# A gated recurrence and a soft mixture of experts: an overlapping last token group, constants and a reciprocal moved later, and a hidden layer in four tiles

## The chip, the cores and the metric

One NeuronCore of a Trainium2 chip. The metric is device time of one execution in microseconds (us). A run over 1.5% above the fastest of its kernel counts as slow. In the views, PE is TensorE, PEld its weight loads, DVE VectorE, ACT ScalarE, POOL GpSimd and SP the queue that issues the loads; PEclk is the clock that TensorE was granted, in tenths of full speed, one digit for each of 40 slices of the span.

## The reference

```python
# x, f_logit: [4, 5056, 256] float32; lower_bound: [256]; phi: [256, 32]; w1: [8, 256, 1024]; w2: [8, 1024, 256]
f = lb + (1 - lb) * sigmoid(f_logit)
h = f[:, t] * h + (1 - f[:, t]) * x[:, t]        # over 5056 tokens, y[:, t] = h
logits = y @ phi                                  # y as 20224 tokens
slot_input = softmax(logits, axis=0).T @ y        # 32 slots, 4 per expert
slot_out[e] = relu(slot_input[e] @ w1[e]) @ w2[e]
out = softmax(logits, axis=1) @ slot_out
```

## The kernel before

Each batch's 5056 tokens are cut into ten groups of 512 (4 tokens a partition, 128 partitions); a group of one batch is a unit, so there are 40. 5056 is 9 x 512 + 448, so the last group fills 112 partitions. Per unit: two loads; a sigmoid (`gate`, ScalarE); its product with x (`enter`, GpSimd); transposes of both (TensorE); the decay (ScalarE); two scans, the recurrence itself (VectorE); transposes back. Groups are exponentiated and gathered into slots in pairs, the last two alone. Expert weights are loaded by GpSimd's queue between its products. In the experts' layer, slot_sb holds the gathered slots, sin the slots made ready for the experts, hi_ps the products of the hidden layer, ht_ps their transposes, so_ps the products of the second layer and slot_out its result.

```python
def rows(g):
    return min(P, (S - g * G) // R)          # 128, and 112 for the last group
# ... constants: ident goes twice through TensorE; rep and phi on VectorE, all ahead of the loop
def load(n):
    g, b = divmod(n, B); n_p = rows(g)
    nc.sync.dma_start(out=fs[n][:n_p], in_=f_logit[b, ds(g * G, n_p * R)]...)   # x_t likewise
# ... the loop over n; in it, in this order on their engines:
    unit(decay, n + 1); group(exps, n - 2); unit(gate, n + 3)      # ScalarE
    unit(enter, n + 3); load_w(...)                                # GpSimd
    unit(to_tokens, n - 1); unit(s_to_channels, n + 2); unit(u_to_channels, n + 1)   # TensorE
    unit(scan, n); ...; group(row_sums, n - 4)                     # VectorE; row sums on GpSimd
nc.vector.tensor_copy(slot_sb, slot_ps)
nc.vector.reciprocal(rrow, rsum)
# ... experts' layer
for q in range(E // Q):
    hi_ps = pbig.tile([P, F], F32, tag=f"hi_ps{q}")                # both halves, one tile
    for k in range(2):
        # 8 matmuls into hi_ps[..., half k]
        if k == 0: nc.scalar.activation(hi[half 0], hi_ps[half 0], ACT.Relu)
        else:      nc.vector.tensor_scalar_max(hi[half 1], hi_ps[half 1], 0.0)
```

The softmax here doesn't subtract the row's maximum and nothing guards it: scores larger than these inputs give would overflow.

## Time and profile before

| | before |
|---|---|
| time, median of 4 runs | 219.65 us (219.25 to 221.96) |
| span of the profiled run | 218.2 us |
| last x load landed | 132.7 us |
| last scan starts | 137.79 us |
| last weight landed | 150.4 us |
| experts' layer, slot_sb to slot_out | 145.69 to 160.54 us |

Times in the second half are from the span's start, in the profiled run. The loads' row carries the first stage, the rows from slot_sb to slot_out a chain in which nearly every instruction waits for the one before, and the output is again a DMA stage. The lines themselves stand in the prediction.

Three measurements of this trace behind the prediction. The page counts 8.39 MB for the 16 weights, 2 bytes an element; of the 58.23 MB read from HBM, 41.42 are the loads of x and f_logit, and the other 16.8 match the weights' float32 size. The packet times of all queues, the weights' among them, sum to 1.01 to 1.07 of the 16 engines in each stretch of 4 us from 112 to 148 us. And unit 35's product ended at 117.33, but its transposes started at 121.92, behind those of unit 36's sigmoid (121.12).

### The profile page before, as it was taken

To read this page: it belongs to the slowest core of one execution; us is meant where nothing else is said; L and a number is where in the kernel's file an instruction comes from. 1 tells how busy PE (TensorE), PEld (TensorE's weight loads), DVE (VectorE), ACT (ScalarE), POOL (GpSimd) and SP (SyncE) were. 2 spreads that over 40 slices of the span, in tenths; PEclk is the share of its full clock that TensorE was granted. 3 is DMA by queue.
4 is the path that set the end of the run, shared out by engine and by line. 5 is a ranking of instruction groups with operands and counts; after the bars stand their busy time and mean duration, and the time that the engine had idled before them with its cause. 6 is when DMAs were issued, how large, how long until landed. Compare 5 with 4: busy or idle time off the path is not lost. (4 is left out here: it accounts for less than half of the span.)

```text
span 218.2 us, 3088 instructions
## 1 busy us (share of the span) xinstructions
PE 133.0 (61%) x1042; PEld 90.8 (42%) x1042; DVE 152.3 (70%) x165; ACT 137.1 (63%) x220; POOL 109.7 (50%) x93
## 2 busy tenths in 40 slices
PE   0386637456664776658573793665958778667600
PEld 0275525355553555556452762432733323223300
DVE  0779998909999899989998297533168446465530
ACT  3499556898889989998787858012034554245520
POOL 1379667359993999969983789742000000000000
PEclk9999999969999999999999589555595555555555
DMA  6999999999999999999999999992009999999995
GB/s 200 414 413 411 321 415 333 404 413 341 390 381 357 414 318 420 320 417 338 399 317 267 243 232 213 197 213 59 5 23 405 405 405 407 400 405 405 405 356 187
DMA packets 19696, 70.76 MB, mean 324 GB/s; under 512 B 2464, under 2 KB 2464, under 8 KB 19680
## 3 DMA queue, kind: packets, MB, share of 16 engines
q1 hardware_dynamic: 17088, 62.14, 74.6%
q0 software_dynamic: 2304, 8.39, 19.2%
q8 instruction: 8, 0.13, 0.2%
q10 hardware_dynamic: 288, 0.03, 0.1%
q14 instruction: 8, 0.07, 0.1%
HBM read 58.23 MB, written 20.71 MB: 362 GB/s over the span
## 5 line engine op out<-in xcount | busy, mean ns | idle before, releaser
L150 POOL TENSOR_TENSOR u_t<-s_t,x_t 128x1024 bf16<-128x1024 bf16 (+1 forms) x39 | 83.4, 2152 | 32.6 <-ACT s_t L144 14.2
L184 DVE TENSOR_TENSOR_SCAN h<-a,h,up 128x512 bf16<-128x512 f32 (+1 forms) x72 | 86.5, 1248 | 0.4 <-PE up L157 0.2
L144 ACT ACTIVATE s_t<-f_t 128x1024 bf16<-128x1024 f32 (+1 forms) x40 | 42.6, 1065 | 18.2 <-DMA f_t<-in_f_logit_dram 18.0
L174 ACT ACTIVATE a<-sp,nomlb 128x512 f32<-128x512 bf16 (+1 forms) x80 | 50.2, 685 | 3.9 <-PE sp L157 3.6
L195 PE MATMUL hp<-ident_f,h 128*128 128x128 f32 (+1 forms) x160 | 30.7, 317 | 34.6 <-DVE ht L204 25.5
L420 ACT ACTIVATE ob<-op,rrow 128x256 f32<-128x256 f32 (+1 forms) x64 | 25.1, 474 | 30.2 <-DVE ob L414 13.1
L414 DVE TENSOR_TENSOR ob<-op,rrow 128x1024 f32<-128x1024 f32 (+1 forms) x24 | 29.0, 1223 | 19.5 <-DMA out_dram<-ob 16.2
L195 PEld LDWEIGHTS hp<-ident_f,h 128*128 128x128 f32 (+1 forms) x160 | 22.6, 208 | 45.5 <-DVE ht L204 34.4
L408 PE MATMUL op<-slot_out,etall 32*128 32x256 bf16 (+1 forms) x160 | 33.9, 379 | 12.4 <-ACT ob L420 7.7
L157 PE MATMUL sp<-ident_f,s_t 128*128 128x128 f32 (+1 forms) x160 | 26.7, 296 | 10.2 <-ACT s_t L144 9.8
L408 PEld LDWEIGHTS <-etall 32*128 32x128 bf16 (+1 forms) x160 | 15.4, 130 | 30.9 <-issue 27.7
L157 PE MATMUL up<-ident_f,u_t 128*128 128x128 f32 (+1 forms) x160 | 26.2, 291 | 2.8 <-POOL u_t L150 2.8
L157 PEld LDWEIGHTS sp<-ident_f,s_t 128*128 128x128 f32 (+1 forms) x160 | 20.5, 155 | 11.9 <-ACT s_t L144 11.0
L157 PEld LDWEIGHTS up<-ident_f,u_t 128*128 128x128 f32 (+1 forms) x160 | 20.5, 153 | 3.4 <-POOL u_t L150 3.3
L204 DVE COPY ht<-hp 128x512 f32<-128x512 f32 (+1 forms) x30 | 20.0, 666 | 1.8 <-PE hp L195 1.8
L243 DVE COPY et<-ep 128x1024 bf16<-128x1024 bf16 (+2 forms) x6 | 3.6, 602 | 15.3 <-PE ep L240 15.3
L184 DVE TENSOR_TENSOR_SCAN h<-a,up 128x512 bf16<-128x512 f32 x8 | 9.1, 1202 | 1.5 <-PE up L157 1.5
L228 ACT ACTIVATE etall<-lg 128x1024 bf16<-128x1024 f32 (+2 forms) x6 | 5.2, 872 | 7.2 <-PE lg L219 7.1
L262 POOL TENSOR_TENSOR rs<-rs 128x128 f32<-128x128 f32 (+6 forms) x18 | 7.9, 442 | 1.4
L144 ACT ACT_TABLE_LOAD x5 | 6.4, 1283 | 3.1 <-PEq L439 1.7
L262 POOL TENSOR_TENSOR rs<-et 128x512 f32<-128x512 bf16 (+2 forms) x6 | 6.0, 998 | 3.8 <-DVE et L243 3.8
L270 PE MATMUL slot_ps<-ht,et 128*32 128x256 bf16 (+1 forms) x160 | 7.4, 314 | 0.6 <-DVE et L243 0.6
(89 smaller groups left out, 92.0 us busy)
## 6 DMA issues: line engine op xcount, KB each, us to landing
f_t<-in_f_logit_dram SPq DMA_DIRECT2D x36, 512.0 KB, 12.5
x_t<-in_x_dram SPq DMA_DIRECT2D x36, 512.0 KB, 12.5
out_dram<-ob SPq DMA_DIRECT2D x36, 512.0 KB, 5.6
f_t<-in_f_logit_dram SPq DMA_DIRECT2D x4, 448.0 KB, 15.6
x_t<-in_x_dram SPq DMA_DIRECT2D x4, 448.0 KB, 16.2
out_dram<-ob SPq DMA_DIRECT2D x4, 448.0 KB, 6.0
w_sb_105<-in_moe_w_dram POOLq DMA_DIRECT2D x1, 512.0 KB, 8.6
w_sb_106<-in_moe_w_dram POOLq DMA_DIRECT2D x1, 512.0 KB, 8.1
```

The costliest lines, as they stand in the source:

```text
L144: nc.scalar.activation(sts[n][:n_p], fs.pop(n)[:n_p], ACT.Sigmoid, scale=-1.0)
L150: eng.tensor_tensor(uts[n][:n_p], sts[n][:n_p], xs.pop(n)[:n_p], ALU.mult)
L157: nc.tensor.transpose(ps[:, :n_p, r], t[:n_p, r], ident_f[:n_p, :n_p])
L174: nc.scalar.activation(a[:, :T], sp[:, :T, o], ACT.Identity, scale=nomlb[:, ds(o, 1)], bias=1.0)
L184: nc.vector.tensor_tensor_scan(h[:, :T, o], decays.pop((n, o))[:, :T], up[:, :T, o], hs[n - B][:, ds(G - 1, 1), o] if n >= B else 0.0, ALU ...
L195: nc.tensor.transpose(hp[:n_p, r], hw[:, :n_p, r], ident_f)
L204: copy(hts[g][:n_p, b].rearrange("p r d -> p (r d)").bitcast(F32), hps.pop(n)[:n_p].rearrange("p r c -> p (r c)"))
L262: nc.gpsimd.tensor_tensor(dst, part[:, :, :w], part[:, :, ds(w, w)], ALU.add)
L270: nc.tensor.matmul(slot_ps[ds(b * NS, NS), :], et[:n_p, r, b], ht[:n_p, b, r], start=(g == 0 and r == 0), stop=(g == n_grp - 1 and r == R ...
L408: nc.tensor.matmul(op[:n_p, r], ew[ds(b * NS, NS), :, r], slot_out[ds(b * NS, NS), :], start=True, stop=True, skip_group_check=True)
L414: nc.vector.tensor_tensor(ob[:n_p], op[:n_p], rrow[:n_p, g, :, ds(b, 1)].broadcast_to([n_p, R, D]), ALU.mult)
L420: nc.scalar.activation(ob[:n_p, r], op[:n_p, r], ACT.Copy, scale=rrow[:n_p, g, r, ds(b, 1)])
```

## The change

The intent: let the last group start at token 4544, overlapping the one ahead by 64 tokens, so that every load fills 128 partitions (of the group ahead only 448 tokens are used); start the first unit before the constants are built; move the reciprocal off the chain; and give each half of the hidden layer a tile of its own. The core of the diff:

```diff
+    def first(g):
+        return g * G if g < n_grp - 1 else S - G
+    def used(g):
+        return first(g + 1) - first(g) if g < n_grp - 1 else G
     def rows(g):
-        return min(P, (S - g * G) // R)
+        return used(g) // R
 ...
-                in_=f_logit[b, ds(g * G, n_p * R)]...        # n_p = rows(g)
+                in_=f_logit[b, ds(first(g), n_p * R)]...     # n_p = P; x_t, gate, enter, transposes, scan likewise
 ...
-                    hs[n - B][:, ds(G - 1, 1), o] if n >= B else 0.0,
+                    hs[n - B][:, ds(used(n // B - 1) - 1, 1), o] if n >= B else 0.0,
 ...
-    # word, word_t: ident by two transposes on TensorE, ahead of the loop
+            if n == -3: lb_constants()          # two small operations
+            if n == 1:  other_constants()       # ident, four copies of rep, two of phi, on VectorE
 ...
-    nc.vector.reciprocal(rrow, rsum)            # ahead of the experts' layer
+        nc.vector.reciprocal(rrow, rsum)        # behind the copies of the transposed hidden layer
 ...
-            hi_ps = pbig.tile([P, F], F32, name="hi_ps", tag=f"hi_ps{q}")
             for k in range(2):
+                hi_ps = pbig.tile([P, H], F32, name="hi_ps", tag=f"hi_ps{q}{k}")
```

More of the change, by code (lines that the diff above doesn't have):

```diff
@@ L50 @@
     make_identity(nc, ident_f)
-    word = consts.tile([P, P, 2], BF16, name="word")
-    nc.vector.memset(word.rearrange("p c o -> p (c o)"), 0.0)
-    nc.vector.tensor_copy(word[:, :, 0], ident_f)
-    word_t = consts.tile([P, P, 2], BF16, name="word_t")
     ident = consts.tile([P, P], BF16, name="ident")
-    with tc.tile_pool(name="psi", bufs=1, space=PSUM) as psi:
-        ip = psi.tile([P, P], F32, name="ip")
-        iw = psi.tile([P, P], F32, name="iw")
-        w_f = word.bitcast(F32).rearrange("p c o -> p (c o)")
-        wt_f = word_t.bitcast(F32).rearrange("p c o -> p (c o)")
-        nc.tensor.transpose(ip, w_f, ident_f)
-        nc.scalar.copy(wt_f, ip)
-        nc.tensor.transpose(iw, wt_f, ident_f)
-        nc.vector.tensor_copy(wt_f, iw)
-        nc.vector.tensor_copy(ident, word_t[:, :, 0])
     rep = consts.tile([P, B, NS], F32, name="rep")
-    for b in range(B):
-        blk = ident_f[ds(b * NS, NS), ds(b * NS, NS)]
-        nc.vector.tensor_copy(rep[ds(b * NS, NS)],
-                              blk.unsqueeze(1).broadcast_to([NS, B, NS]))
     lb = consts.tile([P, DC], F32, name="lb")
@@ L77 @@
     omlb = consts.tile([P, DC], F32, name="omlb")
-    nc.vector.tensor_scalar(omlb, lb, -1.0, 1.0, ALU.mult, ALU.add)
     nomlb = consts.tile([P, DC], F32, name="nomlb")
-    nc.vector.tensor_scalar(nomlb, lb, 1.0, -1.0, ALU.mult, ALU.add)
     phi_f = consts.tile([P, DC, NS], F32, name="phi_f")
@@ L83, with lb_constants, other_constants @@
     phi = consts.tile([P, DC, NS], BF16, name="phi")
-    for o in range(DC):
-        nc.vector.tensor_scalar_mul(phi[:, o], phi_f[:, o], omlb[:, ds(o, 1)])
+    def lb_constants():
+        nc.vector.tensor_scalar(omlb, lb, -1.0, 1.0, ALU.mult, ALU.add)
+        nc.vector.tensor_scalar(nomlb, lb, 1.0, -1.0, ALU.mult, ALU.add)
+    def other_constants():
+        nc.vector.tensor_copy(ident, ident_f)
+        for b in range(B):
+            blk = ident_f[ds(b * NS, NS), ds(b * NS, NS)]
+            nc.vector.tensor_copy(rep[ds(b * NS, NS)],
+                                  blk.unsqueeze(1).broadcast_to([NS, B, NS]))
+        for o in range(DC):
+            nc.vector.tensor_scalar_mul(phi[:, o], phi_f[:, o], omlb[:, ds(o, 1)])
     store = ctx.enter_context(tc.tile_pool(name="store", bufs=1))
@@ L129, in load @@
             g, b = divmod(n, B)
-            n_p = rows(g)
+            n_p = P
             fs[n] = ld.tile([P, R, D], F32, name="f_t", tag="f_t")
@@ L133, in load @@
                 out=fs[n][:n_p],
-                in_=f_logit[b, ds(g * G, n_p * R)].rearrange("(p r) d -> p r d", r=R))
+                in_=f_logit[b, ds(first(g), n_p * R)].rearrange("(p r) d -> p r d", r=R))
             xs[n] = ld.tile([P, R, D], F32, name="x_t", tag="x_t")
@@ L137, in load @@
                 out=xs[n][:n_p],
-                in_=x[b, ds(g * G, n_p * R)].rearrange("(p r) d -> p r d", r=R))
+                in_=x[b, ds(first(g), n_p * R)].rearrange("(p r) d -> p r d", r=R))
         def gate(n):
-            n_p = rows(n // B)
+            n_p = P
             sts[n] = sup.tile([P, R, D], BF16, name="s_t", tag="s_t")
@@ L146, in enter @@
         def enter(n):
-            n_p = rows(n // B)
+            n_p = P
             uts[n] = sup.tile([P, R, D], BF16, name="u_t", tag="u_t")
@@ L152, in to_channels @@
         def to_channels(n, src, dst, tag):
-            n_p = rows(n // B)
+            n_p = P
             t = src[n].bitcast(F32)
@@ L169, in decay @@
         def decay(n):
-            T = rows(n // B) * R
+            T = G
             sp = pss.pop(n)
@@ L178, in scan @@
         def scan(n):
-            T = rows(n // B) * R
+            T = G
             h = hpool.tile([P, G, DC], BF16, name="h", tag="h")
@@ L293 @@
             unit(load, n + AHEAD)
-            unit(decay, n + 1) if n >= 0 else None
+            unit(decay, n + 1)
             group(exps, n - 2)
@@ L299 @@
             unit(enter, n + 3)
+            if n == -3:
+                lb_constants()
+            if n == 1:
+                other_constants()
             for _ in range(W_AT.get(n, 0)):
@@ L306 @@
             unit(u_to_channels, n + 1)
-            if n == -1:
-                decay(0)
             group(logits, n - 1)
@@ L347 @@
         for q in range(E // Q):
-            hi_ps = pbig.tile([P, F], F32, name="hi_ps", tag=f"hi_ps{q}")
             hi = ew.tile([P, F], BF16, name=f"hi{q}")
             for k in range(2):
+                hi_ps = pbig.tile([P, H], F32, name="hi_ps", tag=f"hi_ps{q}{k}")
                 for o in range(DC):
                     for j in range(Q):
-                        nc.tensor.matmul(hi_ps[ds(j * NS, NS), ds(k * H, H)], sin[:, o],
+                        nc.tensor.matmul(hi_ps[ds(j * NS, NS)], sin[:, o],
                                          w1_sb[q * Q + j][:, o, ds(k * H, H)],
@@ L357 @@
                 if k == 0:
-                    nc.scalar.activation(hi[:, ds(k * H, H)], hi_ps[:, ds(k * H, H)], ACT.Relu)
+                    nc.scalar.activation(hi[:, ds(k * H, H)], hi_ps, ACT.Relu)
                 else:
-                    nc.vector.tensor_scalar_max(hi[:, ds(k * H, H)], hi_ps[:, ds(k * H, H)], 0.0)
+                    nc.vector.tensor_scalar_max(hi[:, ds(k * H, H)], hi_ps, 0.0)
             his.append(hi)
@@ L422 @@
             nc.sync.dma_start(
-                out=out[ds(b * S + g * G, n_p * R)].rearrange("(p r) d -> p r d", r=R),
+                out=out[ds(b * S + first(g), n_p * R)].rearrange("(p r) d -> p r d", r=R),
                 in_=ob[:n_p])
```

## The prediction

> **What bounds the kernel now.** I read the page's slices first, then its DMA issues, then the stretches, and last the timeline of the places where the chain of work changes its nature.
>
> The program has three stages. Up to about 149 us it streams x and f_logit (40 units of two 512 KB loads) and 16 expert weights; to about 161 us it runs the experts' layer; then it streams the output. The slices show which is bound by what:
>
> ```profile
> PEclk9999999969999999999999589555595555555555
> DMA  6999999999999999999999999992009999999995
> GB/s 200 414 413 411 321 415 333 404 413 341 390 381 357 414 318 420 320 417 338 399 317 267 243 232 213 197 213 59 5 23 405 405 405 407 400 405 405 405 356 187
> ```
>
> The DMA row stays at 9 from the second slice to the 27th (5 to 147 us), is 0 in two slices (the experts' layer) and 9 again to the end. So the first and last stages are DMA stages and the middle one is a chain through TensorE and its helpers. The bytes tell more. A slice of plain loads runs at 411 to 415 GB/s; a slice with a weight in it shows less because the weight is cast on the way and its float32 reads are not counted. But from slice 21 (115 us) on, the rate is 197 to 267 while the engines are as busy as ever. Some of that is the last eight weights. The rest is this:
>
> ```profile
> f_t<-in_f_logit_dram SPq DMA_DIRECT2D x36, 512.0 KB, 12.5
> ...
> f_t<-in_f_logit_dram SPq DMA_DIRECT2D x4, 448.0 KB, 15.6
> ```
>
> The last token group has 448 tokens, so its loads fill 112 partitions; they are an eighth smaller and take 3.1 us longer. I added up the DMA packets in the trace (one 4 KB packet per partition row): those of the first 72 loads take 163 ns in the mean, those of the eight 112-row loads 265 ns. 896 packets x 265 ns / 16 engines = 14.8 us of all engines, where eight full loads would need 1024 x 160 / 16 = 10.2 us.
>
> The compute behind the loads is nearly as tight:
>
> ```profile
> 80.00:100.00 20.00, 12.51 (x112) 9.89 (x110) 19.20 (x21) 18.55 (x26) 17.31 (x13) 1.00 1.03 387
> ...
> 120.00:125.00 5.00, 3.88 (x22) 3.57 (x23) 1.06 (x2) 4.81 (x8) 3.50 (x3) 0.53 1.04 245
> ```
>
> The columns are PE, PEld, DVE, ACT, POOL, then clock, DMA share, GB/s. VectorE is busy 19.2 of 20 us in a steady stretch (two scans and a copy, 2.94 us a unit), against some 3.2 us of DMA a unit (2.56 for the two loads, 0.65 for a quarter of a weight). Then in 120 to 125 us VectorE falls to 1.06 of 5. The timeline shows the wait:
>
> ```profile
> 118.72 1.28 ACT L144 ACT_TABLE_LOAD   x1 [1.35 <-DMA f_t<-in_f_logit_dram]
> 120.01 1.06 ACT L144 ACTIVATE s_t<-f_t 112x1024 bf16<-112x1024 f32 x1
> ...
> 121.12 1.01 PE L157 MATMUL sp<-ident_f,s_t 112*128 112x112 f32 x4 [3.25 <-ACT s_t L144]
> ...
> 124.55 2.44 DVE L184 TENSOR_TENSOR_SCAN h<-a,h,up 128x512 bf16<-128x512 f32 x2
> ...
> 127.93 2.16 POOL L150 TENSOR_TENSOR u_t<-s_t,x_t 112x1024 bf16<-112x1024 bf16 x1 [1.07 <-DMA x_t<-in_x_dram]
> ...
> 131.18 1.17 POOL L262 TENSOR_TENSOR rs<-et 128x512 f32<-128x512 bf16 x1
> ...
> 134.32 2.14 POOL L150 TENSOR_TENSOR u_t<-s_t,x_t 112x1024 bf16<-112x1024 bf16 x1
> ...
> 137.79 2.18 DVE L184 TENSOR_TENSOR_SCAN h<-a,h,up 128x448 bf16<-128x448 f32 x2
> ```
>
> Unit 36, the first with 112 rows, makes ScalarE wait 1.35 us for its load; TensorE, in order, holds back unit 35's transposes; VectorE stands 5.1 us between the scans of 34 and 35. The last scan starts at 137.79, after GpSimd's last product at 134.32, which itself stood behind row sums and weight issues.
>
> The experts' layer, 145.7 to 161.3 us:
>
> ```profile
> 146.86 1.15 DVE L319 RECIPROCAL rrow<-rsum 128x160 f32<-128x160 f32 x1 [0.75 <-POOL rsum L262]
> 147.93 0.31 DVE L338 TENSOR_SCALAR sin<-sin_ps,omlb 128x32 bf16<-128x32 f32 x2
> ...
> 150.01 0.58 PE L353 MATMUL hi_ps<-w_sb_105,sin 128*32 128x512 bf16 x1 [0.83 <-ACT hi_1821 L358]
> ...
> 152.60 0.59 PE L353 MATMUL hi_ps<-w_sb_109,sin 128*32 128x512 bf16 x1 [0.69 <-ACT hi_1841 L358]
> ```
>
> The reciprocal, needed only by the output stage, stands in front of sin; and the second half of each hidden tile waits until ScalarE has read the first.
>
> [...]
>
> **The change part by part.**
>
> Full loads. The last group starts at token 4544 and overlaps the one ahead by 64 tokens; bytes rise by 0.52 MB, DMA work falls by 14.8 - 10.2 = 4.6 us. So the last weight should land near 145.8 instead of 150.4. The path to the last scan gains less, since other things end the waits:
> - ScalarE: unit 35's load lands at 112.65 as before. After it stand sigmoid (1.06), decay (1.25), two table loads (1.28 each) and the exponential (1.2). Unit 36's sigmoid can start at 118.7, not 120.01: 1.3 us, if its load has landed, which at full rate is about 117.
> - VectorE: that makes the scan of 35 about 123.2; the following at 2.94 us apart reach 132.0 for unit 38, and with its 2.44 us and a 0.42 us copy the last scan could start at 134.9.
> - GpSimd: 119.8 for unit 36, then 2.15, weight issue 0.6, 2.15, 0.6, 2.15, two issues 1.1, row sums 3.2: the last product starts near 131.8 and ends at 133.9; from its end to the scan were 1.33 us, so 135.2.
> So both say 135.0, a gain of 2.8 us. The scan is 512 long instead of 448 (2.44 for 2.18): minus 0.26. Net 2.5.
>
> Start. The identity's two trips through TensorE go, and the first scan, 12.71 us before, can start near 9.3. Then ident, rep and phi (0.23, 0.91, 0.39) come before the second scan: 13.1 for 14.96. But the loads set the pace from unit 7 on, so I count nothing for the end.
>
> Reciprocal behind the hidden copies: sin starts when sin_ps is done, at 147.25 instead of 147.93: 0.7 us. In its new place it has the 2.85 us of the second layer beside it.
>
> Four banks: the two waits go, 0.83 + 0.69 = 1.5 us. [...]
>
> Clock: without those holes [...]the clock may be released before the second layer's 64 matmuls instead of in their middle (five of their eight groups ran at 0.43 us, the last two at 0.22). An estimate: 0.8 us.
>
> Output: same bytes, the four 112-row stores moved from the end into the middle. They cost 194 ns a packet against 164 before; nothing gained or lost.
>
> Sum: 2.5 + 0.7 + 1.5 + 0.8 = 5.5 us; the last weight, at 146, is not late for a second layer starting near 150. 219.74 - 5.5 = 214.2.
>
> **The rivals.**
> A. The whole 4.6 us arrives at the last scan: if GpSimd and VectorE were ahead at unit 35 because of the earlier start. For it: VectorE has little slack, so 2 to 3 us gained early could survive. Against: scans wait for loads at units 7, 8, 27 and 35, which erases a lead. Then 212.4.
> B. The path to the last scan is compute and hides the loads: VectorE needs 2.94 us a unit while four full units arrive every 2.56 us. Weight issues and row sums on GpSimd stay where they are. If 1.3 us of the 2.8 is all, the clock stays low, and the rest holds, the time is 216.5.
> C. The second layer waits for the last weights, because the chain ahead of it gets shorter: four weights are issued only after GpSimd's last product. Against: the DMA queue has work without a break until then, and there are 4 us of room. If it happens, a microsecond is lost.
> D. 128-row loads at the end are as slow as 112-row ones, because the weights beside them are to blame. Against: 100 to 105 us had a weight beside plain loads, and the loads' packets took 167 ns. Then 217.5.
>
> **Range and chances.** The centre is 214.2. The sure parts are 0.7 and 1.5. The load part may be 1.3 to 4.4, the clock 0 to 1.3. All low gives 216.2, all high 211.8; I take 212.4 to 216.1. Two per cent is 215.35. That is 1.1 us from my centre, somewhat over one of the errors I expect: 0.8 for faster, 0.19 for the same, 0.01 for slower.
>
> **What would show it.** Right: the f_t issues all 512 KB near 12.5 us to landing at the end; the wait of ScalarE for unit 36's load gone; last scan near 135; no wait of hi_ps on ScalarE; sin directly behind sin_ps; slot_out near 155 instead of 160.06; output stage 57.5 us long as before. Wrong: if the last loads' packets stay above 200 ns (D); if scan 39 starts after 136.5 with VectorE busy throughout (B) or before 134 (A); if the second layer's matmuls wait for a weight (C); if the output stage changes by over 1 us.

## The result, and the profile after

213.87 us (median of 4 runs, 213.70 to 214.48) against 219.65; the ratio is 0.9721 (95% interval 0.9651 to 0.9791). All ratios here are the mean time of one kernel's fast runs over that of the other's of the same rounds, so not quite the ratio of the medians quoted.

The slices of the changed kernel, and its f_t loads:

```profile
PEclk9998599987999699999999999555965555555555
DMA  6999999999999999999999999993049999999994
GB/s 201 416 410 408 317 420 408 321 419 379 345 416 320 419 327 404 368 367 415 317 419 327 405 290 205 177 214 66 5 172 407 404 406 404 405 404 406 343 364 186
...
f_t<-in_f_logit_dram SPq DMA_DIRECT2D x40, 512.0 KB, 12.5
```

Slices are 5.3 us now. The plain-load rate holds to the 23rd (405 GB/s, 117 to 122 us); only the tail of weights after it shows less. The packets of the last eight loads take 162 ns (265 before), the last x load lands at 126.5 (132.7) and the last weight at 146.6 (150.4).

The same places of the timeline as in the prediction (start, duration, engine, line, operation):

```profile
116.96 1.28 ACT L141 ACT_TABLE_LOAD   x1
118.25 1.06 ACT L141 ACTIVATE s_t<-f_t 128x1024 bf16<-128x1024 f32 x1
...
121.62 2.45 DVE L181 TENSOR_TENSOR_SCAN h<-a,h,up 128x512 bf16<-128x512 f32 x2
...
131.21 2.13 POOL L147 TENSOR_TENSOR u_t<-s_t,x_t 128x1024 bf16<-128x1024 bf16 x1
...
135.38 2.45 DVE L181 TENSOR_TENSOR_SCAN h<-a,h,up 128x512 bf16<-128x512 f32 x2
...
145.31 0.41 DVE L335 TENSOR_SCALAR sin<-sin_ps,omlb 128x32 bf16<-128x32 f32 x2 [1.22 <-PE sin_ps L331]
...
151.04 1.14 DVE L377 RECIPROCAL rrow<-rsum 128x160 f32<-128x160 f32 x1
```

The wait for the load has gone from the table load's line: the sigmoid of unit 36 now follows the exponential without a hole. The last scan is 2.41 us earlier. The reciprocal now stands beside the second layer, and sin starts 0.10 us after sin_ps ends (0.69 before).

The chain of waits through the experts' layer, before (start, duration, what):

```profile
148.14 1.07 PE hi_ps L353 x8
...
150.01 1.92 PE hi_ps L353 x15
...
152.60 1.04 PE hi_ps L353 x8
...
154.17 1.80 PE ht_ps L368 x16
155.97 2.85 PE so_ps L387 x33
```

and after:

```profile
145.61 3.60 PE hi_ps L350 x32
...
149.53 0.54 PE ht_ps L365 x8
...
150.11 0.68 PE ht_ps L365 x8
150.79 1.89 PE so_ps L385 x64
```

The three pieces of hi_ps have become one, and the transposes and the second layer are shorter too: the trace's clock records give full speed from 149.1 us, before the transposes; in the kernel before it came at 157.9, in the middle of the second layer.

Where the 5.5 us of span went, along this path (starts are the timeline's, which can be some hundredths before the chain's):

| stretch | before | after | gain |
|---|---|---|---|
| span's start to last scan | 137.79 | 135.38 | 2.41 |
| last scan to slot_sb | 7.90 | 8.28 | -0.38 |
| slot_sb to sin | 2.24 | 1.65 | 0.59 |
| sin to first hi_ps | 0.21 | 0.30 | -0.09 |
| hi_ps, first start to last end | 5.51 | 3.60 | 1.91 |
| to the first so_ps | 2.25 | 1.50 | 0.75 |
| to slot_out | 4.16 | 3.20 | 0.96 |
| slot_out to the end | 58.16 | 58.76 | -0.60 |

### The profile page after: what moved, and what is told of

Its sections match the earlier page's. It is cut to its first block, busy times and chain, and to the rows that moved or that the text cites.

```text
span 212.7 us, 3083 instructions
## 1 busy us (share of the span) xinstructions
PE 132.1 (62%) x1040; PEld 91.6 (43%) x1040; DVE 155.9 (73%) x162; ACT 137.5 (65%) x219; POOL 109.6 (52%) x93
## 5 line engine op out<-in xcount | busy, mean ns | idle before, releaser
L147 POOL TENSOR_TENSOR u_t<-s_t,x_t 128x1024 bf16<-128x1024 bf16 x39 | 83.4, 2153 | 29.6 <-ACT s_t L141 20.7
L181 DVE TENSOR_TENSOR_SCAN h<-a,h,up 128x512 bf16<-128x512 f32 x72 | 87.6, 1265 | 0.0
L192 PE MATMUL hp<-ident_f,h 128*128 128x128 f32 (+1 forms) x160 | 31.8, 326 | 40.3 <-DVE ht L201 34.6
L171 ACT ACTIVATE a<-sp,nomlb 128x512 f32<-128x512 bf16 x80 | 50.7, 690 | 7.7 <-PE sp L154 7.7
L141 ACT ACTIVATE s_t<-f_t 128x1024 bf16<-128x1024 f32 x40 | 42.6, 1064 | 6.2 <-DMA f_t<-in_f_logit_dram 6.2
L154 PE MATMUL sp<-ident_f,s_t 128*128 128x128 f32 x160 | 27.4, 299 | 11.0 <-ACT s_t L141 11.0
L154 PE MATMUL up<-ident_f,u_t 128*128 128x128 f32 x160 | 26.6, 293 | 2.1 <-POOL u_t L147 2.1
L154 PEld LDWEIGHTS sp<-ident_f,s_t 128*128 128x128 f32 x160 | 21.1, 157 | 12.6 <-ACT s_t L141 6.5
L154 PEld LDWEIGHTS up<-ident_f,u_t 128*128 128x128 f32 x160 | 20.9, 154 | 2.4 <-POOL u_t L147 2.2
L201 ACT COPY ht<-hp 128x512 f32<-128x512 f32 (+1 forms) x10 | 5.8, 582 | 5.9 <-PE hp L192 5.9
```

The lines of the kernel that those rows point to most:

```text
L141: nc.scalar.activation(sts[n][:n_p], fs.pop(n)[:n_p], ACT.Sigmoid, scale=-1.0)
L147: eng.tensor_tensor(uts[n][:n_p], sts[n][:n_p], xs.pop(n)[:n_p], ALU.mult)
L154: nc.tensor.transpose(ps[:, :n_p, r], t[:n_p, r], ident_f[:n_p, :n_p])
L171: nc.scalar.activation(a[:, :T], sp[:, :T, o], ACT.Identity, scale=nomlb[:, ds(o, 1)], bias=1.0)
L181: nc.vector.tensor_tensor_scan(h[:, :T, o], decays.pop((n, o))[:, :T], up[:, :T, o], hs[n - B][:, ds(used(n // B - 1) - 1, 1), o] if n >= ...
L192: nc.tensor.transpose(hp[:n_p, r], hw[:, :n_p, r], ident_f)
```

## The experiments

The theory: the overlap removes the slow 112-row loads and gives some 2 us; the reciprocal gives 0.6; four tiles give their two waits and an earlier clock. Rivals: the start carries the gain; the weights make the last loads slow; the load's 4.6 us arrive in full. Each kernel gives the reference's result.

**The parts alone.** Four kernels on one chip, against the kernel before.

Only the overlap (`first`, `used`, 128-row loads, as in the diff):

> The kernel before with the overlapping last group alone. Theory: [...]only about 2 us reach the end, because the sigmoid of unit 36 then waits for the exponential and its table loads, not for the load. Packets of the last eight loads near 162 ns instead of 265, last load landed near 126 instead of 132.7, slot_sb near 143.7 instead of 145.7; time 217.6, ratio 0.991. Rival A (all 4.6 us arrive): 215.1, ratio 0.979. Rival D (the weights beside them are to blame): packets stay above 230 ns, ratio 1.00.

0.9916 (0.9889 to 0.9944), median 218.11. Packets of the last loads 162 ns, last x load landed at 126.05, last scan at 135.45, slot_sb at 142.94. This is the expected 0.991; rivals A and D are out.

Everything but the overlap:

```diff
-        return g * G if g < n_grp - 1 else S - G
+        return g * G                            # and 112-row loads for the last group
```

> The changed kernel without the overlap (last group with 112 rows again). Theory, additive: what is left is the reciprocal (0.6), the two waits of hi_ps (1.5 to 1.9) and the earlier release of the TensorE clock (up to 1.8): 3.7 us, 215.9, ratio 0.983. If instead the loads and the rest only help together, this one stays within 1 us of before.

0.9790 (0.9756 to 0.9825), 214.94 us: somewhat more than the expected 0.983. The profiled run's last loads took 251 ns a packet, and its last scan was 0.8 us earlier than before's, which may be that difference. From hi_ps's first start to slot_out's it took 8.22 us, as the changed kernel does (8.31). The parts add: 0.9916 x 0.9790 = 0.971, and 0.972 was measured. So of the 28 thousandths some 8 are the overlap's and 21 the rest: of 219.65 us, 1.8 us and 4.6 us, where the prediction had 2.5 and 3.0.

Only the four tiles:

> The kernel before with the hidden layer in four banks alone. Waits alone: from the first matmul of hi_ps to the first of so_ps 7.8 us before becomes 6.2, time 218.1, ratio 0.993. Waits and clock: 5.2 to 5.5 us, the second layer 1.9 us instead of 2.9, time 216.3, ratio 0.985.

0.9891 (0.9853 to 0.9929), 217.26 us. The ratio lies between the two forecasts and doesn't settle it; the trace does: hi_ps to so_ps took 4.77 us and the second layer's matmuls 1.93 (2.88 before), so waits and clock, not waits alone. The total gain of 2.4 us is less than the 3.5 us by which slot_out was earlier in the profiled run, which was itself a quick one (216.67).

Only the reciprocal:

```diff
-    nc.vector.reciprocal(rrow, rsum)            # ahead of the experts' layer
+        nc.vector.reciprocal(rrow, rsum)        # behind the hidden copies
```

> The kernel before with the reciprocal of the row sums moved behind the hidden copies alone. Theory: sin starts 0.6 us earlier and the rest follows: 219.05, ratio 0.997. Rival (hidden by another wait, or repaid where the reciprocal now stands): 1.000.

0.9930 (0.9894 to 0.9966), but this number misleads. One run, at 215.96 us, was 2.3 us quicker than the next, so the rule of 1.5% counts 15 of the 22 runs as slow, the profiled one (219.61) among them, and the ratio rests on the quickest seven. The means of all runs are 219.36 against 219.88, a ratio of 0.998, near the expected 0.997; by time alone, half a microsecond barely stands out from the noise. The trace is sharper: slot_sb to sin took 1.64 us instead of 2.24.

The tiles, the reciprocal (at 0.998) and the start (0.9998, below) multiply to 0.987, and all of them together gave 0.979. Most of the missing 1.7 us is at a place that none of them touches: in the profiled runs the last scan started at 137.0 with all of them and at 138.2 with the tiles alone. Why is open.

**The start.** Only the start of the change:

> The kernel before with the start of the change alone. Theory: worth nothing at the end (ratio 1.000 within 0.002), since loads and the wait of ScalarE for the logits of the first pair of groups erase a lead or a lag by unit 12. In the start it makes the second scan later (18.7 instead of 15.0), because seven copies of VectorE stand beside GpSimd's products and take 5.8 us instead of 1.5. If the start carried the gain (rival A), ratio 0.99.

0.9998 (0.9968 to 1.0027). The second scan starts at 18.75 instead of 14.96, that of unit 8 at 38.64 instead of 35.04, that of unit 12 at 51.25 instead of 52.32, and nothing is left of either at the end. Rival A, in the form that the start carries the gain, falls.

The start was however not as predicted (second scan 13.1). VectorE in the changed kernel, and below it GpSimd:

```profile
12.92 0.74 DVE L76 CAST ident<-ident_f 128x128 bf16<-128x128 f32 x1
13.59 2.87 DVE L79 COPY rep<-ident_f 32x128 f32<-32x128 f32 x4
16.46 2.29 DVE L82 TENSOR_SCALAR phi<-phi_f,omlb 128x32 bf16<-128x32 f32 x2
18.67 2.32 DVE L181 TENSOR_TENSOR_SCAN h<-a,up 128x512 bf16<-128x512 f32 x2
```

```profile
13.99 2.14 POOL L147 TENSOR_TENSOR u_t<-s_t,x_t 128x1024 bf16<-128x1024 bf16 x1 [0.42 <-DMA x_t<-in_x_dram]
16.58 2.13 POOL L147 TENSOR_TENSOR u_t<-s_t,x_t 128x1024 bf16<-128x1024 bf16 x1 [0.45 <-DMA x_t<-in_x_dram]
```

The copies took 5.8 us, not the 1.5 that the same shapes took before GpSimd's first product. Taken one by one, four of the seven took 0.21 to 0.24 us, as they had there. The time is in the other three: ident ended 0.08 us after the product then running, and two that began within 0.05 us of a product's start ended 0.08 and 0.04 us after its end:

```profile
14.04 2.18 DVE L79 COPY rep<-ident_f 32x128 f32<-32x128 f32 x1
...
16.62 2.13 DVE L82 TENSOR_SCALAR phi<-phi_f,omlb 128x32 bf16<-128x32 f32 x1
```

In the kernel before, the one such copy from SBUF beside a product, ident's at 9.76, took 1.42 us and ended 0.08 us after the product did. By these ends, such copies may be waiting for GpSimd's product. To test this, the same seven on ScalarE:

```diff
-        nc.vector.tensor_copy(ident, ident_f)      # rep and phi likewise
+        nc.scalar.copy(ident, ident_f)
```

> The changed kernel with ident, rep and phi built on ScalarE instead of VectorE. If the 5.8 us of these copies are a wait of VectorE for GpSimd[...], they take some 0.1 to 0.4 us each on ScalarE, the second scan starts near 13.5 instead of 18.7, and the scans up to unit 10 are 3 to 5 us earlier; the end is the same (ratio to the changed kernel 1.00, to before 0.974). If VectorE's copies are slow by themselves, ScalarE's need not be faster, and nothing is told of GpSimd. If the lag at the start reached the end, the time falls by over 1 us.

```profile
16.33 0.28 ACT L76 CAST ident<-ident_f 128x128 bf16<-128x128 f32 x1
16.52 1.22 ACT L79 COPY rep<-ident_f 32x128 f32<-32x128 f32 x4
17.75 0.54 ACT L82 ACTIVATE phi<-phi_f,omlb 128x32 bf16<-128x32 f32 x2
```

Together 2.0 us, and each of those beside a product of GpSimd took 0.30 to 0.32 us; the second scan at 13.37, unit 8's at 34.47 (38.57 in the changed kernel). The ratio is 0.9725 (0.9666 to 0.9783), as the changed kernel's: 4 us of lead at unit 8 buy nothing at the end. That these copies wait for GpSimd is thus supported by when they end and by what ScalarE does; by what means they wait no run shows.

**The 112 rows.** The changed kernel with the short loads one group earlier, all of the last group full:

```diff
-            n_p = P
+            n_p = rows(n // B)                  # 112 for the group ahead of the last
```

> The changed kernel, but the group before the last loads only the 112 rows that are used, so no byte is loaded twice and the short loads come where almost only plain loads are in flight. If 112 rows are slow by themselves, the packets of these eight loads take 250 to 270 ns, and DMA has 4.6 us more to do: between the two kernels, 215 to 216.5. If the weights or the end of the stream made them slow (rival D), packets near 165 ns and 213.7.

The packets of these eight loads took 277 ns, those after them 163. So it is the 112 rows, not the weights or the place. But the time was 0.9938 (0.9914 to 0.9962), 219.53 us, not 215 to 216.5: the expectation had not worked out where the loss lands. Unit 35's f load lands at 118.17 instead of 112.21, and ScalarE's 6 us of work between it and unit 36's sigmoid comes after that, so the last scan is at 140.71, all of 5.3 us later (277 ns x 896 / 16 - 10.2 = 5.3):

```profile
140.71 2.45 DVE L181 TENSOR_TENSOR_SCAN h<-a,h,up 128x512 bf16<-128x512 f32 x2
```

In the kernel before, the short loads came while ScalarE was in that work, and half was hidden.

The row counts by themselves, in one kernel: groups 1, 3, 5 and 7 in two transfers each.

```diff
+    CUTS = {1: (64, 64), 3: (96, 32), 5: (112, 16), 7: (120, 8)}
```

> The changed kernel with the loads of four groups cut into two transfers each: 64 and 64 rows, 96 and 32, 112 and 16, 120 and 8. A measure of the packets by themselves. [...]If it is [...]a size that is not a power of two, 64 and 32 rows run at 160 like 128 and 96 and 112 do not.

A single run, 242.8 us, of unknown state, so only packets are read. Groups 0, 2, 4, 6, 8 and 9, all in 128 rows, take 162 to 182 ns. 64 + 64 rows take 275, 96 + 32 take 267, 112 + 16 take 254 and 120 + 8 take 229 (means of both parts). 64 rows are a power of two, yet at 275 ns they are as slow: a row count that is not a power of two is not needed for it. Why the packets of loads with fewer than 128 rows take longer no run shows.

**What sets the last scan.** The changed kernel with the row sums of the last pair behind GpSimd's last product:

```diff
+            if n - 6 == 7 * B + B - 1:
+                row_sums(7)                     # at the end of GpSimd's list for this n
 ...
-            group(row_sums, n - 4)
+            if n - 4 != 7 * B + B - 1:
+                group(row_sums, n - 4)
```

> The changed kernel with the row sums of the last pair of groups behind GpSimd's last product instead of ahead of it. If GpSimd's queue sets the last scan, it starts at 133.3 instead of 135.4 (then VectorE's own row of scans sets it) and the time falls by 2 us: 211.8, ratio 0.964. If it is the load or VectorE, nothing changes: 0.974.

GpSimd's last product and VectorE's last scan in it:

```profile
128.87 2.16 POOL L147 TENSOR_TENSOR u_t<-s_t,x_t 128x1024 bf16<-128x1024 bf16 x1
```

```profile
133.92 2.45 DVE L181 TENSOR_TENSOR_SCAN h<-a,h,up 128x512 bf16<-128x512 f32 x2
```

0.9647 (0.9607 to 0.9688) against before, where the changed kernel has 0.9721. The last product starts 2.3 us earlier, the last scan 1.5: from there VectorE's own row of scans holds it. So in the changed kernel GpSimd's queue is the last wait. VectorE's row would have allowed some 133.1 there: 121.62 for unit 35's scan and the 11.50 us from that scan to the last one in this run.

**The clock.** The changed kernel with 22 matmuls of 512 columns whose result nobody reads, in holes of TensorE from 131 us on:

```diff
+        def keep_warm(k):
+            ps = psu.tile([P, P, R], F32, name="sp", tag="sp")
+            for _ in range(k):
+                nc.tensor.matmul(ps..., ident, etall[:, ds(0, G)], start=True, stop=True)
```

> The changed kernel with 22 matmuls that nobody reads (512 columns each) in the holes of TensorE between the last loads and the experts' layer. If the clock at half from 132 to 149 us costs time, and these keep it at full, hi_ps takes 1.9 us instead of 3.6 and the five short steps before it 0.3 to 0.4 us less each: time 210.8 to 212, ratio 0.960 to 0.965. If the clock doesn't bound these steps or the filler delays them by as much: 213.9, 0.974.

```profile
PEclk9999999999999999999999979999975555555555
...
144.06 1.91 PE L361 MATMUL hi_ps<-w_sb,sin 128*32 128x512 bf16 x32 [0.40 <-DVE sin L346]
```

0.9551 (0.9519 to 0.9583), 210.8 us. The clock stays whole from 123.0 to 153.7 us and hi_ps takes 1.91 us instead of 3.60, slot_sb is reached 1.2 us earlier. The gain over the changed kernel, 17 thousandths or 3.7 us, is more than the ratio expected (the time, 210.8, is at the edge of its range): the half clock cost more than the row sums did.

Both:

> Both: 209 to 210.5, ratio 0.952 to 0.958, if the two gains lie one after the other on the same path.

0.9521 (0.9485 to 0.9556), 209.97 us: the row sums' 7 thousandths are nearly lost beside the filler. In the trace, the last product is early (128.17), but its transposes stand behind eight filler matmuls until 133.37, and the last scan starts at 134.99. A last run moved the filler:

```diff
-                keep_warm(8)                    # between the product and its transposes
+                keep_warm(4)                    # one step earlier
```

> Both again, with the eight filler matmuls that stood between the last product and its transposes replaced by four in a hole one step earlier (20 in all? no: 4 + 7 + 3 + 2 + 2 = 18). In the run of both, the transposes of the last product waited behind the filler and the last scan started at 135.0 instead of 133.9. If that is why the two gains did not add, the last scan starts at 133.9 or earlier and the time falls by 1.1 us against the run of both: ratio 0.947. If the clock drops for want of the eight, hi_ps takes over 2.5 us and the ratio is 0.95 to 0.955.

0.9503 (0.9456 to 0.9550), 209.55 us, hi_ps 1.91 us. The last scan came at 134.56, not 133.9. The delay was there by unit 35: from its scan to the last it took 11.50 us, as with the late row sums, but from the sigmoid of unit 36 to that scan 4.65 us instead of 3.36, with the clock at half from 118 to 125 us. It is not told apart from the run of both (0.9521); that the filler in the way was the whole reason stays open. It is the quickest version, and both it and the run of both beat the two kernels.

## Why the prediction was right

It said 214.2 and 213.87 came. By its steps:

- **Full loads.** DMA work fell as worked out (packets 162 ns for an expected 160; last weight at 146.6 for 145.8). The step that mattered, that only part of 4.6 us reaches the last scan, held: sigmoid 118.25 for 118.7, GpSimd's last product 131.21 for 131.8, scan 135.38 for 135.0. Rival A fell with the overlap alone (0.9916), rival D with the shifted short group (277 ns), and rival B with the 2.41 us at the scan. But "both say 135.0" was not so. Unit 35's scan came at 121.62 for 123.2: from the sigmoid of unit 36 to it took 3.37 us, at full clock, for 4.54 before, mostly at half clock (0.5 from 120.35). VectorE's row was therefore 2 us ahead, and GpSimd alone set the scan. With the overlap alone unit 35's scan came at 123.51, and the last at 135.45 all the same. GpSimd's product began 0.6 us earlier than said, and from its end to the scan took 2.04 us, at half clock, for 1.33: two errors that nearly cancel. The longer last scan was put at 0.26; scan to slot_sb cost 0.38.
- **Start.** Zero at the end, as said. The way there failed: the first scan came at 10.67 for 9.3, and "13.1 for 14.96" was 18.67. I had taken the copies' durations from a place where GpSimd was idle.
- **Reciprocal.** 0.7 said, 0.59 in the trace; the time of the part alone barely tells it from zero.
- **Four tiles (its "four banks").** 1.5 said, 1.91 measured for hi_ps. The holes between the three pieces were 0.80 and 0.67 us, 1.5 in all; the rest is that the pieces took 4.03 us and the one piece takes 3.60. Why is not shown.
- **Clock.** That full speed comes earlier was right and the size was not: 0.8 said, 0.75 + 0.96 = 1.7 measured, as it came 3.5 us after hi_ps's start, before the transposes; the prediction had hoped only for "before the second layer". Over the runs, with four tiles it came 2.8 to 5.8 us after the start, with two 8.3 to 10.0 (9.8 in the kernel before, where the clock had been at half from 137.4). So part of the 1.7 is this run's: with the copies on ScalarE it came 5.8 us after, and from hi_ps's end to so_ps took 2.19 us instead of 1.50. With the filler, the clock's weight is shown directly; what exactly releases it no run shows.
- **Output.** Said to be the same; it was 0.6 longer in the profiled run. Over all profiled runs, slot_out's end to the span's end was 57.5 to 58.1 us in the five kernels with the 112-row stores at the end; with them in the middle it was 58.3 to 58.7 in four and 57.5 to 57.9 in the four with late row sums or filler. The moved stores may cost half a microsecond in the first four; no run tests it.
- **Rival C** did not come: the last weight landed 4 us before the second layer.

Tiles and clock together gave 1.3 us more than said, the output stage and small terms took it back; and by the runs of the parts alone the overlap gave less than said (1.8 for 2.5) and the rest more (4.6 for 3.0). The nearness of the total is partly luck, and the range was the honest part. Rival D's 217.5 also left out the clock's 0.8; by the prediction's own terms it was 216.7.

## What to carry to other kernels

Before pricing a slow transfer, ask what stands between it and the end: the same 112-row loads cost 2 us where a busy engine hid half, and all 5 us one group earlier. Here it paid to let every load fill all 128 partitions (162 ns a packet, against 265 for 112 rows), though 64 tokens of each batch are loaded twice. In a chain of short TensorE steps look at the granted clock: filling the holes with matmuls that stand in nobody's way was worth more here (3.7 us) than the waits that the four tiles removed (1.5).

## What the runs measured of the hardware

- Packets of loads, 4 KB each: 112 rows 249 to 277 ns in six kernels, against 162 for 128 rows; 64 + 64 rows 275; 96 + 32 rows 267; 120 + 8 rows 229.
- TensorE was busy 4.29 of 5 us (150 to 155 us, kernel before) at half clock, with holes of 0.83 us just before and 0.69 us in it; with filler, busy 3.63 to 4.42 of each 5 us from 130 to 150 us, it stayed at full. So the busy share of such stretches does not tell the two apart.
